# Hedgehog attention and an ELU layer on one core: the first batch written in beats, all five engines in program order

## The chip, the core and the metric

The kernel runs on one core of one Trainium2 chip. The core has five engines with a queue each: TensorE (PE; its weight loads are shown apart as PEld), VectorE (DVE), ScalarE (ACT), GpSimd (POOL) and SyncE (SP), which here only issues transfers. Transfers are carried by DMA engines that all queues share. The metric is the device time of one launch in microseconds; lower is better.

## The reference

For 8 batches and 8 heads, with 576 tokens of 64 features each, q and k are projected with one weight matrix to 128 features. The largest absolute value of each token's projection is subtracted before both exponentials are taken. An output token is a quotient of two sums over the keys. The result goes, as 4608 tokens of 512 features, through a layer of 2048 hidden units with an ELU.

```python
def phi(x):
    proj = np.einsum('bhsd,df->bhsf', x, w_phi)
    proj = proj - np.max(np.abs(proj), axis=-1, keepdims=True)
    return np.concatenate([np.exp(proj), np.exp(-proj)], axis=-1)
q_p, k_p = (phi(q), phi(k))
kv = np.einsum('bhsf,bhsd->bhfd', k_p, v)
z = np.sum(k_p, axis=2)
num = np.einsum('bhsf,bhfd->bhsd', q_p, kv)
den = np.einsum('bhsf,bhf->bhs', q_p, z)[..., None] + 1e-06
...
h = x @ w_in
g = np.where(h > 0.0, h, alpha * (np.exp(np.minimum(h, 0.0)) - 1.0))
return (g @ w_out).astype(np.float32)
```

q, k and v are 8 x 8 x 576 x 64, w_phi 64 x 128, w_in 512 x 2048, w_out 2048 x 512, all float32; the kernel computes its matrix products in bfloat16.

## The kernel before

**Attention in quads.** A quad is four heads of a batch: 512 tokens of each as "main" part, 64 as "tail". There are 16 quads, two per batch, called q0 to q15 here. `attention_steps(i)` returns the steps of quad i: `tr` brings k and q to feature-major order (tiles kT and qT; for i < 3 by TensorE transposes and a copy out of PSUM, for later quads by transposing DMAs on SP's queue); `k` projects the keys of one head at a time (PSUM tile pk), DVE takes the largest absolute value (m_k), ACT the two exponentials (EK); `scale` and `vs` scale the values by exp of m_k (em, vs); `q` does the largest value for the queries (m_q); `qf` their exponentials (Eq); `kv` multiplies EK and vs; `out` multiplies Eq and kv, and DVE combines the two signs (tot); the last out step also divides (den, rec, x); `x` brings x to feature-major order for the layer (xT, and xT_tail for the tails).

**The layer in pieces.** A chunk is the 512 main tokens of a batch; a ninth chunk holds all tails. `mm1(ch, jt)` makes one of 16 column tiles of the hidden layer: four matmuls into PSUM (ph), then ACT's exp (e_sb), POOL's subtraction (u_sb) and DVE's min and max (gT). `mm2(ch, tt, part)` makes a quarter of the product for one of four token tiles tt: four matmuls into PSUM (po); after the fourth quarter ACT copies po to o_sb and SP stores it. The list `pieces` holds them in order, 32 per chunk: 16 mm1 with the last 8 quarters (tt 2 and 3) of the chunk before put in between, then the 8 quarters of tt 0 and 1. A chunk's pieces begin when its number is in `ready`.

**Two regimes.** Quads q0 and q1 and the transposes of q2 are written as one list of steps before manual scheduling starts. There `post` runs its function at once, and the framework's scheduler decides the order on each engine. From q2 on the kernel is in beats: the order on all engines is the program's. Each beat writes one piece of the layer and the steps that `slot_beats` gives it; 16 beats make a slot, a slot holds the k and q half of one quad and the kv and out half of the quad before. `post(lag, fn, rank)` puts work on another engine some beats later, sorted by rank within a beat. Chunk 0 is ready at the first beat, chunk 1 at the 52nd.

**PSUM.** There are eight banks: four for attention (`apsum`, tag ap), three for ph (`mpsum`, tag mp), one for po (`opsum`, tag op). The next po can start only when ACT has copied the last one.

**Loads.** k, q, w_in and w_out are loaded by POOL's queue, which casts to bfloat16; v of batch 0 by POOL too, later v by SP. In the trace an issue on POOL waits for the eighth issue before it to land.

Of the kernel before, what the change touches and what calls it, by code (L numbers as in the profile page):

```python
# [8 lines left out]
FP32 = mybir.dt.float32  # L9
# [13 lines left out]
def kernel(  # L23
# [104 lines left out]

    beat = [0]
    agenda = {}  # L130
    in_beats = [False]
# [15 lines left out]
    def attention_steps(i):  # L147
# [3 lines left out]
        def transposes(n):  # L151
# [4 lines left out]
            if i < 3:  # L156
                tr = apsum.tile([P, 8, P], BF16, name="tr", tag="ap")
# [3 lines left out]
                copy = nc.scalar.copy if n == 1 and b == 0 else nc.vector.tensor_copy  # L161
                copy(dst[:, 0:8, :], tr)
                trt = apsum.tile([P, P], BF16, name="trt", tag="ap")
                nc.tensor.transpose(trt, src[:, t0:t0 + P], ident)
                copy(dst[:, 8, :], trt)
# [14 lines left out]
        def project(xT, hh, m):  # L180
# [4 lines left out]
            for j in range(n):  # L185
# [9 lines left out]
                1,  # L195
# [21 lines left out]
        def k_head(hh):  # L217
            pk = project(st["kT"], hh, st["m_k"])
            if hh < 4:
                exps(pk, lambda sg: st["EK"][:, hh, sg, :], 2)  # L220
            else:
                exps(pk, lambda sg: st["EKt"][:, sg, :], 2)

        def q_head(hh):
            project(st["qT"], hh, st["m_q"])


        eng = nc.vector if i == 1 else nc.gpsimd

        def k_scale():  # L230
# [6 lines left out]
            eng.tensor_copy(vs[:, :, :, D], em)  # L237

        def v_scaled(sg, c):
# [7 lines left out]
            eng.tensor_tensor(  # L247
# [17 lines left out]
        def q_features_tail():  # L265
# [13 lines left out]
            def weights():  # L279
                st["w"] = small.tile([P, 2 * NS], FP32, name="w")  # L280
                nc.scalar.activation(st["w"], st["m_q"], ACT.Exp, scale=2.0)

            post(2, weights, 6)
# [92 lines left out]
        def divide():  # L376
# [5 lines left out]
            for c in range(2):  # L382
                r = slice(c * NS, (c + 1) * NS)
                nc.vector.tensor_tensor(  # L384
                    st["x"][:, :, c, :],
                    st["tot"][:, r, 0:D],
                    rec[:, r, None].to_broadcast((P, NS, D)),
                    op=ALU.mult,
                )

        def x_out():
# [11 lines left out]
            tr = apsum.tile([P, 8, P], BF16, name="tr", tag="ap")  # L403
            for j in range(8):
                nc.tensor.transpose(tr[:, j, :], x[:, j * P:(j + 1) * P], ident)
            nc.vector.tensor_copy(main, tr)
# [267 lines left out]
```

## Time and profile before

| | |
|---|---|
| time, median of 3 runs | 448.89 us (445.23 to 450.13) |
| time of the profiled execution | 446.22 us |
| its span | 444.4 us |
| PE busy | 378.0 us (85%) |
| DVE busy | 284.5 us (64%) |
| ACT busy | 266.7 us (60%) |
| POOL busy | 213.3 us (48%) |
| read from HBM, written to it | 36.77 MB, 9.44 MB |

The profile shows one execution: busy time per engine, the span in 40 slices of 11.1 us with each engine's busy share in tenths, the TensorE clock that was granted, DMA traffic, and groups of instructions with what ended the idle time before them. A row of the timeline begins with start and duration in us. A row of a table by stage has the stage, its length, and for each engine the busy time and the number of instructions, then the granted clock, the DMA engines' busy share and GB/s.

### The profile page before, as it was taken

Reading aid. Unit: us, or ns where it says so; the run is one execution under the profiler, and the core shown is the slowest. Engines: PE = TensorE matmul, PEld = TensorE weight load, DVE = VectorE, ACT = ScalarE, POOL = GpSimd, SP = SyncE. Lnnn points to the kernel's source line nnn. Section 1 sums busy time; section 2 is a strip of 40 time slices with the busy share of each in tenths; the row PEclk is TensorE's granted clock in tenths of the full one; section 3 lists DMA queues with packets and bytes.
Section 4 is the critical chain, followed back from the end, with each engine's and each line's share of the span. In section 5 each row is a group of like instructions: output and inputs, shape, how many; then the busy total and the mean of one; then the engine's idle time right before and its main releaser. Section 6 shows DMA issues by size and latency. Waiting matters only on the chain.

```text
span 444.4 us, 7930 instructions
## 1 busy us (share of the span) xinstructions
PE 378.0 (85%) x2888; PEld 203.7 (46%) x2888; DVE 284.5 (64%) x552; ACT 266.7 (60%) x585; POOL 213.3 (48%) x325
## 2 busy tenths in 40 slices
PE   2575687965989898989898989898999899989985
PEld 2353434543545454535454545454555444434432
DVE  2665676767597768765977687768776763523410
ACT  2953187766668576857685768486848533434511
POOL 9562177544186527742774277436434621423400
PEclk9955699995899999999999999999999999999999
DMA  8899995099309972994199419941521202010023
GB/s 135 158 172 212 226 153 78 23 125 204 70 11 178 159 125 24 108 232 107 21 182 155 112 29 202 139 103 43 63 62 39 50 25 75 27 47 24 25 53 65
DMA packets 93720, 44.89 MB, mean 101 GB/s; under 512 B 62545, under 2 KB 88273, under 8 KB 93681
## 3 DMA queue, kind: packets, MB, share of 16 engines
q1 hardware_dynamic: 65136, 29.57, 33.3%
q0 software_dynamic: 28544, 14.82, 25.2%
q8 instruction: 22, 0.36, 0.3%
q14 instruction: 18, 0.14, 0.1%
HBM read 36.77 MB, written 9.44 MB: 104 GB/s over the span
## 4 chain that ended last, share of the span: by engine, by line
PE 63%; DVE 13%; ACT 11%; DMA 5%; issue 4%; POOL 3%; POOLq 0%; ACTq 0%
PE ph L436 24%; PE po L469 23%; PE pk L186 5%; ACT Eq L212 4%; PE pkv L293 4%; DMA qT<-q_b 4%; DVE x L384 3%; ACT EK L212 3%; DVE gT L455 3%; PE pq L256 2%; ACT o_sb L479 2%; PE pn L326 2%; PE pkv L305 1%; DVE m_q L196 1%; DVE m_k L196 1%
## 5 line engine op out<-in xcount | busy, mean ns | idle before, releaser
L448 POOL TENSOR_SCALAR u_sb<-e_sb 128x512 bf16<-128x512 f32 x144 | 91.4, 636 | 161.9 <-ACT e_sb L445 155.6
L469 PE MATMUL po<-w_out_sb,gT 128*128 128x512 bf16 x576 | 142.4, 379 | 12.2 <-ACT o_sb L479 12.2
L436 PE MATMUL ph<-xT,w_in_sb 128*128 128x512 bf16 x512 | 131.6, 384 | 15.8 <-DVE gT L455 15.4
L445 ACT ACTIVATE e_sb<-ph 128x512 f32<-128x512 f32 x144 | 87.0, 606 | 68.0 <-PE ph L436 65.8
L455 DVE SCALAR_TENSOR_TENSOR gT<-u_sb,ph 128x512 bf16<-128x512 bf16 x144 | 97.4, 682 | 44.0 <-POOL u_sb L448 43.2
L469 PEld LDWEIGHTS <-gT 128*128 128x128 bf16 x576 | 55.4, 98 | 70.2 <-issue 16.1
L436 PEld LDWEIGHTS <-w_in_sb 128*128 128x128 bf16 x576 | 54.3, 98 | 71.1 <-issue 23.5
L212 ACT ACTIVATE Eq<-pq 128x512 bf16<-128x512 f32 x128 | 68.9, 605 | 29.6 <-PE pq L256 29.0
L196 DVE TENSOR_REDUCE m_k<-pk 128x4 f32<-128x512 f32 (+1 forms) x80 | 50.3, 635 | 45.0 <-PE pk L186 44.8
L212 ACT ACTIVATE EK<-pk 128x512 bf16<-128x512 f32 x128 | 69.7, 624 | 11.5 <-DVE m_k L196 11.3
L247 POOL TENSOR_TENSOR vs<-v_b,em 128x512 bf16<-128x512 f32 (+1 forms) x90 | 72.9, 827 | 0.0
L196 DVE TENSOR_REDUCE m_q<-pk 128x4 f32<-128x512 f32 (+1 forms) x80 | 50.6, 635 | 26.4 <-PE pk L186 26.4
L479 ACT COPY o_sb<-po 128x512 f32<-128x512 f32 x36 | 21.3, 591 | 40.0 <-PE po L469 34.3
L186 PE MATMUL pk<-w_phi_both,qT 128*128 128x256 bf16 x144 | 30.8, 290 | 8.2 <-DMA qT<-q_b 4.3
L186 PE MATMUL pk<-w_phi_both,kT 128*128 128x256 bf16 x144 | 30.4, 289 | 5.6 <-DVE m_q L196 2.0
L326 PEld LDWEIGHTS <-Eq 128*128 128x128 bf16 x512 | 25.9, 101 | 16.8 <-issue 4.6
L338 DVE TENSOR_TENSOR tot<-pn,w 128x260 f32<-128x260 f32 x64 | 27.1, 425 | 9.7 <-ACT kv L313 5.1
L326 PE MATMUL pn<-kv,Eq 128*128 128x65 bf16 x512 | 28.6, 199 | 3.1 <-DVE tot L338 1.3
L344 DVE TENSOR_TENSOR tot<-tot,pn 128x260 f32<-128x260 f32 x64 | 27.0, 425 | 1.9
L256 PE MATMUL pq<-qT,w_phi_both 128*128 128x512 bf16 x64 | 25.2, 407 | 0.6 <-ACT Eq L212 0.6
L293 PEld LDWEIGHTS <-EK 128*128 128x128 bf16 x512 | 21.6, 102 | 6.7 <-ACT EK L212 2.3
L186 PEld LDWEIGHTS <-kT 128*128 128x128 bf16 x144 | 14.7, 103 | 20.0 <-issue 6.5
(61 smaller groups left out, 263.2 us busy)
## 6 DMA issues: line engine op xcount, KB each, us to landing
out_dram<-o_sb SPq DMA_DIRECT2D x32, 256.0 KB, 2.4
v_b<-in_v_dram SPq DMA_DIRECT2D x7, 1024.0 KB, 10.6
k_b<-in_k_dram POOLq DMA_DIRECT2D x7, 512.0 KB, 7.9
q_b<-in_q_dram POOLq DMA_DIRECT2D x7, 512.0 KB, 12.0
w_in_sb<-in_moe_w_in_dram POOLq DMA_DIRECT2D x8, 256.0 KB, 7.6
w_out_sb<-in_moe_w_out_dram POOLq DMA_DIRECT2D x8, 256.0 KB, 16.7
v_b<-in_v_dram POOLq DMA_DIRECT2D x2, 512.0 KB, 6.5
out_dram<-o_sb SPq DMA_DIRECT2D x8, 128.0 KB, 2.4
```

The source lines that it names most:

```text
L186: nc.tensor.matmul(pk[:, 2 * j:2 * j + 2, :].rearrange("p a b -> p (a b)"), xT[:, 2 * hh + j, :], w_phi_rhs, start=True, stop=True,)
L196: lambda: nc.vector.tensor_reduce(m[:, o:o + NT] if hh < 4 else m[:, NS - 1::NS], pk[:, 0:2 * n, :], axis=AX.X, op=ALU.max, apply_absolute ...
L212: lambda sg=sg: nc.scalar.activation(dst(sg), psum, ACT.Exp, scale=1.0 - 2.0 * sg),
L247: eng.tensor_tensor(st["vs"][:, sg, r, 0:D], kqv[b][2][:, o:o + n * D].rearrange("p (n d) -> p n d", d=D), st["em"][:, sg, r, None].to_bro ...
L256: nc.tensor.matmul(pq, w_phi_both[:, par, :], st["qT"][:, 4 * c:4 * c + 4, :].rearrange("p a b -> p (a b)"), start=True, stop=True,)
L293: nc.tensor.matmul(pkv[:, c, sg, :], st["EK"][:, 2 * c + s, sg, t * F:(t + 1) * F], st["vs"][:, sg, c * NS + s * NT + t, :], start=first, ...
L326: nc.tensor.matmul(pt[:, t, :], st["Eq"][:, par, c, sg, o:o + P], st["kv"][:, s, c, sg, :], start=True, stop=True,)
L436: nc.tensor.matmul(ph, w_in_sb[:, ct, jt * P:(jt + 1) * P], xTs[ch][:, ct, :] if ch < B else xT_tail[:, ct // 2, :, ct % 2, :], start=(ct ...
L445: post(1, lambda: nc.scalar.activation(e_sb, ph, ACT.Exp), 0)
L448: lambda: nc.gpsimd.tensor_scalar(u_sb, e_sb, -1.0, 1.0, op0=ALU.add, op1=ALU.mult),
L455: lambda: nc.vector.scalar_tensor_tensor(gTs[ch][:, jt, :], u_sb, 0.0, ph, op0=ALU.min, op1=ALU.max),
L469: nc.tensor.matmul(po, gTs[ch][:, jt, tt * P:(tt + 1) * P], w_out_sb[:, jt, :], start=(jt == 0), stop=(jt == N_JT - 1),)
```

## The change

The first three quads are written in beats too, and manual scheduling starts before the first instruction. The hand-written table gives each step of q0 to q2 a beat: the slot of q3 starts at beat 39, chunk 0 is ready at beat 29 and chunk 1 at beat 75, where the beats before q2's slot had no number in the kernel before. From the slot of q4 on the table is the old one.

- Chunk 0 has eight more empty places in the list of pieces, one behind each mm2 quarter.
- w_in is loaded in eight parts as before, but each part is one half of the columns for two row tiles. Batch 0's second k half is loaded ahead of q and v.
- kT and qT of q3 and q4 are made by TensorE and a copy, as those of q0 to q2 are; their PSUM tiles lie in the ph or po banks. The copies of q0's and q1's qT are DVE's and no longer ACT's; q2's kT copy and q0's xT copy are ACT's and no longer DVE's.
- For q0 and q1 the exponentials of a key head stand one beat ahead of its largest value, no longer behind it.
- vs of q1 is POOL's work and no longer DVE's. x of q0 (the two multiplications behind the division) is POOL's, a beat after the division.
- po of tt 1 lies in a ph bank. When attention is over, all po lie in the four attention banks.

```diff
-    def load_w_in(ct, c):
+    def load_w_in(half, g, c):
+        j = slice(half * (DFF // 2), (half + 1) * (DFF // 2))
         nc.gpsimd.dma_start(
-            out=w_in_sb[c * D:(c + 1) * D, ct, :], in_=w_in_r[ct // 2, c, ct % 2]
+            out=w_in_sb[c * D:(c + 1) * D, 2 * g:2 * g + 2, j],
+            in_=w_in_r[g, c, :, :, j].rearrange("s d j -> d s j"),
         )
...
     def post(lag, fn, rank=5):
-        if in_beats[0]:
-            agenda.setdefault(beat[0] + lag, []).append((rank, fn))
-        else:
-            fn()
+        agenda.setdefault(beat[0] + lag, []).append((rank, fn))
...
-            if i < 3:
-                tr = apsum.tile([P, 8, P], BF16, name="tr", tag="ap")
+            if i < 5:
+
+                pool, tag = (opsum, "op") if i in (2, 3) else (mpsum, "mp")
+                tr = pool.tile([P, 8, P], BF16, name="tr", tag=tag)
...
+                copy = nc.scalar.copy if i == 2 and n == 0 else nc.vector.tensor_copy
+                post(1, lambda: copy(dst[:, 0:8, :], tr), 0)
+                post(1, lambda: copy(dst[:, 8, :], trt), 0)
...
         def k_head(hh):
-            pk = project(st["kT"], hh, st["m_k"])
+
+            lag = 2 if i < 2 else 1
+            pk = project(st["kT"], hh, st["m_k"], lag)
             if hh < 4:
-                exps(pk, lambda sg: st["EK"][:, hh, sg, :], 2)
+                exps(pk, lambda sg: st["EK"][:, hh, sg, :], 3 - lag)
...
-        eng = nc.vector if i == 1 else nc.gpsimd
...
-            eng.tensor_tensor(
+            nc.gpsimd.tensor_tensor(
                 st["vs"][:, sg, r, 0:D],
...
-            for c in range(2):
...
+            def x_heads():
+                for c in range(2):
+                    r = slice(c * NS, (c + 1) * NS)
+                    (nc.gpsimd if i == 0 else nc.vector).tensor_tensor(
...
+            if i == 0:
+                post(1, x_heads, 8)
+            else:
+                x_heads()
...
         if part == 0:
-            pos[ch, tt] = opsum.tile([P, DM], FP32, name="po", tag="op")
+
+            pool, tag = opsum, "op"
+            if not attending[0]:
+                pool, tag = apsum, "ap"
+            elif tt == 1:
+                pool, tag = mpsum, "mp"
+            pos[ch, tt] = pool.tile([P, DM], FP32, name="po", tag=tag)
...
-        pieces += [(ch, tt, part) for tt in (0, 1) for part in range(4)]
+        for tt in (0, 1):
+            for part in range(4):
+                pieces.append((ch, tt, part))
+                if ch == 0:
+                    pieces.append(None)
...
+    put(0, (16, 17, 18, 19, 20), q0["out"])
...
+    put_later(0, (29,), [lambda: ready.add(0)], 1)
...
+    put_later(0, (1, 2), load_kq(1, 0), 9)
+    put_later(0, (3, 4, 13, 13), w_in_loads[0], 9)
+    put_later(0, (18,), [hold_v], 9)
+    put_later(0, (19,), [lambda: load_v(1)], 9)
+    put_later(0, (20, 21), load_kq(1, 1), 9)
+    put_later(0, (23, 24, 25, 26), w_in_loads[1], 9)
+    put_later(0, (28, 29, 30, 31), w_out_loads[:4], 9)
+    put_later(0, (38, 40, 42, 44), w_out_loads[4:], 9)
...
+    START = 39
...
```

On POOL's queue before, from the third w_in load to the first work of the layer, vs is that of q0 only, and all loads of batch 1 and of w_out stand in a row:

```order
L81 DMA w_in_sb<-in_moe_w_in_dram 64x2048 x3
L237 CAST vs<-em 128x36
L247 TENSOR_TENSOR vs<-v_b,em 128x8x64 x4
L247 TENSOR_TENSOR vs<-v_b,em 128x2x64
L81 DMA w_in_sb<-in_moe_w_in_dram 64x2048
L247 TENSOR_TENSOR vs<-v_b,em 128x2x64
L81 DMA w_in_sb<-in_moe_w_in_dram 64x2048 x4
L107 DMA k_b<-in_k_dram 128x8x256
L117 DMA k_b<-in_k_dram 64x4x64 x2
L107 DMA q_b<-in_q_dram 128x8x256
L117 DMA q_b<-in_q_dram 64x4x64 x2
L86 DMA w_out_sb<-in_moe_w_out_dram 128x2x512 x8
```

The same place on POOL's queue after the change, from q1's em on:

```order
L236 CAST vs<-em 128x36
L246 TENSOR_TENSOR vs<-v_b,em 128x2x64
L82 DMA w_in_sb<-in_moe_w_in_dram 64x2x1024 x2
L246 TENSOR_TENSOR vs<-v_b,em 128x8x64 x4
L246 TENSOR_TENSOR vs<-v_b,em 128x2x64 x2
L109 DMA q_b<-in_q_dram 128x8x256
L119 DMA q_b<-in_q_dram 64x4x64 x2
L383 TENSOR_TENSOR x<-tot,rec 128x9x64 x2
L82 DMA w_in_sb<-in_moe_w_in_dram 64x2x1024 x4
L88 DMA w_out_sb<-in_moe_w_out_dram 128x2x512 x3
L454 TENSOR_SCALAR u_sb<-e_sb 128x512
L88 DMA w_out_sb<-in_moe_w_out_dram 128x2x512
```

The vs of q1 and the x of q0 have come onto POOL, between loads, and the last loads stand among the layer's u_sb.

On DVE before, from the first m_q of q1 to the middle of q0's out steps, the names with numbers are the PSUM tiles of one out step:

```order
L196 TENSOR_REDUCE m_q<-pk 128x4
L237 CAST vs<-em 128x36
L585 COPY v_b<-em 128x1 x2
L247 TENSOR_TENSOR vs<-v_b,em 128x8x64
L338 TENSOR_TENSOR tot<-pn_384,w 128x260
L196 TENSOR_REDUCE m_q<-pk 128x4
L344 TENSOR_TENSOR tot<-tot,pn_379 128x260
L338 TENSOR_TENSOR tot<-pn_402,w 128x260
L247 TENSOR_TENSOR vs<-v_b,em 128x8x64
L344 TENSOR_TENSOR tot<-tot,pn_397 128x260
```

On DVE after the change, from the end of q0's out steps into those of q1:

```order
L341 TENSOR_TENSOR tot<-tot,pn_438 128x260
L362 TENSOR_TENSOR tot<-pnt,w 128x2x65
L368 TENSOR_TENSOR tot<-tot,pnt 128x2x65
L376 TENSOR_SCALAR den<-tot 128x18
L377 RECIPROCAL rec<-den 128x18
L335 TENSOR_TENSOR tot<-pn_546,w 128x260
L341 TENSOR_TENSOR tot<-tot,pn_541 128x260
```

The vs and the m_q of q1 no longer stand among q0's out steps, and between the division of q0 and the first out step of q1 no x stands on DVE; `tot` has one buffer, so that step waits for POOL's x.

On PE before, in the steady part, where token tile 0 of a chunk ends and token tile 1 begins (with the engines that a row waits for):

```order
L268 LDWEIGHTS w_phi_both
L268 MATMUL pq<-qT,w_phi_both 128x128 [waits Activation_49]
L268 LDWEIGHTS w_phi_both
L268 MATMUL pq<-qT,w_phi_both 128x128
L469 LDWEIGHTS gT
L469 MATMUL po<-w_out_sb,gT 128x512 [waits Activation_49]
```

The same place on PE after the change:

```order
L267 LDWEIGHTS w_phi_both
L267 MATMUL pq<-qT,w_phi_both 128x128 [waits Activation_49]
L267 LDWEIGHTS w_phi_both
L267 MATMUL pq<-qT,w_phi_both 128x128
L482 LDWEIGHTS gT
L482 MATMUL po<-w_out_sb,gT 128x512
```

The order is the same, and the first matmul of tile 1 no longer waits for ACT.

More of the change, by code (lines that the diff above doesn't have):

```diff
@@ L581, in load_v @@
[L581 to L590 removed]
+    w_in_loads = [
+        [
+            lambda half=half, g=g, c=c: load_w_in(half, g, c)
+            for g in range(2)
+            for c in range(2)
+        ]
+        for half in range(2)
@@ L642 @@
+    last = max(at)
+    while beat[0] <= last or pieces or agenda:
+        if beat[0] > last:
+            attending[0] = False
+            if B - 1 in ready:
+                ready.add(B)
+        moe_piece()
+        for f in at.get(beat[0], []):
+            f()
         next_beat()
-        moe_piece()
 _INS = ['q', 'k', 'v', 'w_phi', 'moe_w_in', 'moe_w_out']
```

222 lines of the change are left out of this document (107 added, 115 removed).

## The prediction

> **What bounds the kernel now.** I read the slices of the page first, then the busy time by stage.
>
> ```profile
> span 444.4 us, 7930 instructions
> PE   2575687965989898989898989898999899989985
> PEclk9955699995899999999999999999999999999999
> core 0: us, PE busy (x) PEld busy (x) DVE busy (x) ACT busy (x) POOL busy (x), PEclk, DMA share, GB/s
> 0.00:54.20 54.20, 29.88 (x282) 20.82 (x283) 30.01 (x70) 23.65 (x55) 28.21 (x47) 0.74 1.06 179
> 54.20:91.70 37.50, 31.99 (x222) 16.66 (x220) 25.73 (x48) 27.54 (x62) 25.86 (x39) 0.96 0.64 85
> 91.70:113.80 22.10, 13.84 (x139) 8.61 (x138) 17.22 (x36) 13.12 (x33) 7.18 (x11) 0.72 1.12 177
> 201.20:245.00 43.80, 40.78 (x339) 22.39 (x338) 33.22 (x66) 31.22 (x70) 24.28 (x36) 1.00 0.68 119
> 372.90:444.40 71.50, 62.83 (x286) 27.82 (x285) 22.02 (x32) 25.08 (x43) 19.75 (x32) 0.99 0.15 45
> ```
>
> From the eleventh slice on PE is at 8 or 9 tenths; in the first ten (111 us) it is mostly at 5 to 7. The fourth stage is one steady batch: PE busy 40.78 of 43.80 us (93%). The last stage is the tail, with PE as the bound. The first three stages are the ramp, where no engine is a bound: PE 75.7 of 113.8 us, DVE 73.0, ACT 64.3. The timeline gives its marks:
>
> ```profile
> 6.68 0.69 DVE L162 COPY kT<-tr 128x1024 bf16<-128x1024 bf16 x1 [2.81 <-PE tr L160]
> 54.24 1.06 PE L436 MATMUL ph<-xT,w_in_sb 128*128 128x512 bf16 x2
> 113.75 0.61 PE L436 MATMUL ph<-xT,w_in_sb 128*128 128x512 bf16 x1
> ```
>
> DVE's work starts at 6.7 us, the layer in earnest at 54.2 us (chunk 0, beat 1), and chunk 1 at 113.75 us (beat 52). From chunk 1 on the table of beats is the same in both kernels. The ramp's term is therefore where chunk 1's first ph (now beat 75) falls.
>
> **The ramp.** DVE has most to do once its order is free of waits, so I count DVE's work up to chunk 1: 30.01 + 25.73 + 17.22 = 72.96 us before. Rows of DVE and ACT in the first stage price what moves:
>
> ```profile
> L384 DVE TENSOR_TENSOR x<-tot,rec 128x576 bf16<-128x576 f32 x4 | 2.9, 755 | 0.1
> L247 DVE TENSOR_TENSOR vs<-v_b,em 128x512 bf16<-128x512 f32 x4 | 2.7, 687 | 0.0
> L247 DVE TENSOR_TENSOR vs<-v_b,em 128x128 bf16<-128x128 f32 x2 | 0.6, 297 | 0.0
> L162 DVE COPY kT<-tr 128x1024 bf16<-128x1024 bf16 x3 | 2.1, 688 | 2.9 <-PE tr L160 2.8
> L165 DVE COPY kT<-trt 128x128 bf16<-128x128 bf16 x3 | 0.7, 219 | 0.8 <-PE trt L164 0.8
> L162 ACT COPY qT<-tr 128x1024 bf16<-128x1024 bf16 x2 | 2.0, 1012 | 8.3 <-PE tr L160 8.1
> ```
>
> - q1's vs leaves DVE: 2.7 + 0.6 = -3.3 us. x of q0 leaves it: half of four, -1.5 us.
> - A pair of copies (main and tail) is 0.69 + 0.22 = 0.91 us. q0's and q1's qT come from ACT (+1.8), q3's and q4's kT and qT come from the transposing DMAs (+3.6), q2's kT and q0's xT go to ACT (-1.8).
> - Sum: 72.96 - 3.3 - 1.5 + 1.8 + 3.6 - 1.8 = 71.8 us. ACT exchanges two pairs of copies for two, so its 64.3 us stay.
>
> Now the share of the time in which DVE can work. The ends are a steady batch, where PE sets the pace (33.22 of 43.80: 76%), and the best ramp stretch:
>
> ```profile
> 30.00:40.00 10.00, 4.61 (x43) 3.29 (x43) 8.80 (x23) 0.22 (x1) 3.52 (x5) 0.50 1.32 224
> 60.00:70.00 10.00, 8.23 (x40) 3.77 (x39) 6.79 (x12) 9.47 (x23) 9.46 (x15) 1.00 1.39 171
> 90.00:100.00 10.00, 6.42 (x80) 3.95 (x79) 7.06 (x14) 6.13 (x15) 3.94 (x6) 1.00 1.20 136
> 100.00:110.00 10.00, 5.95 (x49) 3.08 (x46) 8.09 (x18) 6.43 (x17) 4.95 (x7) 0.58 1.08 213
> ```
>
> DVE reached 88% at 30 to 40 us, and 68% at 60 to 70 us, where ACT was full (9.47 of 10). The new order mixes both kinds of work, so I take the steady batch's 76%, the nearest row to mixed work: 6.7 + 71.8 / 0.76 = 101.2 us. That gains 113.75 - 101.2 = 12.6 us. At 88% chunk 1 would start at 88.3 us (gain 25.5). A second way to count comes near it. For chunk 0's start, beat 29:
>
> ```profile
> 0.74 1.28 ACT L162 ACT_TABLE_LOAD   x1 [0.74 <-PEq L658]
> 9.08 1.03 PE L160 MATMUL tr<-ident,q_b 128*128 128x128 bf16 x8 [0.93 <-DMA q_b<-in_q_dram]
> ...
> 11.41 4.03 ACT L212 ACTIVATE EK<-pk 128x512 bf16<-128x512 f32 x8
> 45.33 0.68 PE L326 MATMUL pn<-kv,Eq 128*128 128x65 bf16 x16 [0.62 <-ACT kv L313]
> ```
>
> ACT had 23.65 - 1.28 = 22.4 us of work for the first two quads. Its first exponential at 11.4 us stood behind a qT copy (1.0 us for its main part) and q's transposes (1.0 us); without them it starts at about 9 and ends near 32 us. q1's out steps, division, x and transposes took from 45.3 to 54.2 us, 9 us; with 2 us for POOL's x, below, chunk 0 starts at about 43 us. The 32 beats of the second stage took 37.5 us, 1.17 each, so 46 more give 43 + 53.9 = 97 us.
>
> What the ramp adds in waits:
>
> - `tot` has one buffer, so DVE's first out step of q1 waits for POOL's x of q0, which stands behind three loads of q. DVE's queue holds q1's whole out part behind it, and chunk 0 waits for that. The row for POOL work of this kind is
>
> ```profile
> L247 POOL TENSOR_TENSOR vs<-v_b,em 128x512 bf16<-128x512 f32 x12 | 12.2, 1039 | 0.0
> ```
>
>   Two of 576 elements: 2 x 1.04 x 576/512 = 2.3 us, against 1.5 us on DVE. It lies in the 24% that I leave idle; without that cover it costs 0.8 us.
> - q3's and q4's transposes add four of these pairs to PE, which has 75.7 us of work in 101 us:
>
> ```profile
> 15.67 0.61 PE L160 MATMUL tr<-ident,q_b 128*128 128x128 bf16 x8
> 16.11 0.22 PE L164 MATMUL trt<-ident,q_b 128*128 128x128 bf16 x1
> ```
>
>   4 x (0.61 + 0.22) = 3.3 us, taken at nothing; 3.3 us if PE were full.
> - w_in's loads have the same bytes. The first half's last parts are issued at beat 13 and needed at beat 29, the second half's at beats 23 to 26 and needed at the ninth mm1, beat 41. Taken at nothing, with 15 beats of attention as cover; beyond that cover each us of lateness is one of chunk 0.
> - A key head's exponentials one beat ahead of its largest value, for q0 and q1, changes which of ACT and DVE reads pk first: the same instructions, taken at nothing, and either way within the share.
> - The transposing DMAs that go (q3, q4) free SP; those of q5 stay, and with them this wait:
>
> ```profile
> 101.67 0.53 SPq L107 DMA_DIRECT2D v_b<-in_v_dram  x1
> 110.63 0.61 PE L186 MATMUL pk<-w_phi_both,qT 128*128 128x256 bf16 x2 [3.34 <-DMA qT<-q_b]
> ```
>
>   From the issue of v to the matmul are 9 us. The two are ten beats apart in both kernels, so at 1.17 us a beat most of the 3.3 us goes, and at 0.9 it stays. I leave it inside the share.
>
> **The po banks.** In a steady batch PE waits for ACT's copy of po twice where mm2 quarters follow each other, and six times in the tail:
>
> ```profile
> L479 ACT COPY o_sb<-po 128x512 f32<-128x512 f32 x36 | 21.3, 591 | 40.0 <-PE po L469 34.3
> ...
> 190.74 1.02 PE L469 MATMUL po<-w_out_sb,gT 128*128 128x512 bf16 x4 [0.66 <-ACT o_sb L479]
> 196.18 1.02 PE L469 MATMUL po<-w_out_sb,gT 128*128 128x512 bf16 x4 [0.57 <-ACT o_sb L479]
>   ACT o_sb L479: 4.1, 6
> ```
>
> The first is token tile 3 to tile 0, both still in the po bank: it stays. The second is tile 0 to tile 1: it goes, six times between chunk 1 and chunk 7. PE is busy 93% there, but other waits can take the place, above all this one for gT:
>
> ```profile
> 175.84 1.02 PE L436 MATMUL ph<-xT,w_in_sb 128*128 128x512 bf16 x4 [1.59 <-DVE gT L455]
> ```
>
> So 6 x 0.57 = 3.4 us at most, none at least; I take 2.7. In the tail nothing but PE is late: with four banks the copy of 0.59 us hides behind 16 matmuls, and all 4.1 us go.
>
> **The sum** is made against the profiled execution, 446.22 us: -12.6 - 2.7 - 4.1 = 426.8 us. The three timed runs have a median of 448.89, and all four times average 447.6, 1.4 above the profiled one; so I forecast 428 us.
>
> **The rivals.**
>
> *Dense ramp.* DVE reaches the 88% of its best stretch: 446.2 - 25.5 - 6.8 + 1.4 = 415 us. For it: ACT and PE have 64 and 79 us in 88. Against: that stretch had ACT at 0.22 of 10.
>
> *The ramp at the steady pace.* A steady beat is 43.80 / 32 = 1.37 us, though PE's load makes it so; 75 of them: 6.7 + 102.8 = 109.5 us, a gain of 4.3, and 446.2 - 4.3 - 6.8 + 1.4 = 436.5 us. For it: the order on each engine is fixed, so a beat costs its fullest engine, and POOL has new work. Against: ramp beats hold no or half the layer's pieces.
>
> *The clock stays low.* In the rows by 10 us the granted clock is 1.00 where PE was busy 6.42 or 8.23 of 10, and 0.50 or 0.58 where it was busy 4.61 or 5.95. A ramp cut into short beats with waits in each could keep PE below that. PE's work from beat 29 to 75 is at full clock about 31.99 x 0.96 + 13.84 x 0.72 = 40.7 us, at half clock 81 us: chunk 1 at 43 + 81 = 124 us, and the time 446.2 + 10.3 - 6.8 + 1.4 = 451 us. Against: 40.7 us in the 58 us from 43 to 101 are 7.0 of 10, above both rows with full clock's lower one. The Trainium skill, page "TensorE: Matmul & The Clock Gate", Part 1, says that the clock has two states only, half and full, and falls back after an idle window of about 3.4 us. By that rule intermediate values are mixtures of time, and the waits of a beat, of which the longest steady one shown is 1.59 us, would not trip it; the forecast stands by the rule as by the rows.
>
> *POOL stalls the layer (the slower side).* Each load on POOL waits for the eighth before it to land, and after the change u_sb, without which no gT and no next ph comes, stands behind the last w_out and batch 2's loads on that queue. Before, the loads waited with nothing behind them:
>
> ```profile
> POOL w_out_sb L86 <- DMA q_b<-in_q_dram: 6.8, 3, 5.4
> POOL w_out_sb L86 <- DMA k_b<-in_k_dram: 3.5, 3, 2.7
> ```
>
> If five of the loads behind beat 19 (there are 21) waited like the longest, 5.4 us, on the path, chunk 1 would start 27 us later than forecast, at 128 us: 446.2 + 14.5 - 6.8 + 1.4 = 455 us. It decides from 12.6 + 6.8 + 4.5 = 24 us of such waits on. Against: these waits came where the DMA engines were full (224 GB/s at 30 to 40 us), with all loads issued at once; now they stand over 50 beats.
>
> *The banks do nothing* (PE still waits for ACT in the tail, the copies come late for another reason): 4.1 + 2.7 us less gain, 434 us.
>
> **How the numbers follow.** Forecast, 420 to 433 us: 0.50. Dense ramp: 0.16. Steady pace: 0.18. Low clock: 0.05. POOL's waits: 0.06. Banks alone failing: 0.05. The range holds the forecast, the dense ramp and the steady pace with a margin of some 3 to 4 us for the run-to-run spread: 412 to 440 us. What a measurement of this kernel can tell from no change is about 1%, 4.5 us. Faster by more: 0.50 + 0.16 + 0.18 + 0.05, less 0.03 for a ramp that is slower still than the steady pace: 0.86. The low clock lies within 1%, with that 0.03: 0.08. Slower: 0.06.
>
> **What would show it.** Chunk 1's first ph at 96 to 106 us and chunk 0's at 40 to 46 us; PE's slices 3 to 9 at 7 or more; DVE's busy time up to chunk 1 near 72 us; no wait of po for ACT in the tail and one, not two, per steady batch; the clock at 0.9 or more from 45 us on. Wrong: chunk 1 later than 110 us, POOL loads with waits of over 2 us and u_sb behind them, clock below 0.7 in chunk 0, or ph waits that grow where the po waits went.

## The result and the profile after

The changed kernel takes 426.92 us, median of 4 runs (425.63 to 428.95), against 448.48 us (445.23 to 450.13) of the kernel before on the same chip: a ratio of 0.9532, 95% interval 0.9466 to 0.9598. The forecast was 428 us. One execution of run 2 below took 498.44 us at a mean granted clock of 0.75, and that run's time and ratio are those of its other five. The changed kernel's profiled execution took 426.87 us. Its page, with PE and the granted clock in 40 slices of 10.6 us:

```profile
span 425.1 us, 7945 instructions
PE   3685878767989998999899989998999898999995
PEclk9887899996999999999999999999999899999999
```

PE's slices 3 to 9 read 8, 5, 8, 7, 8, 7, 6 (7, 5, 6, 8, 7, 9, 6 before). Two of them are below the 7 that was forecast: the ramp is shorter, not dense. The stages of the ramp, cut at the new marks (columns as in the prediction's table):

```profile
0.00:43.10 43.10, 27.50 (x280) 18.48 (x281) 27.60 (x63) 26.09 (x59) 32.55 (x51) 0.86 0.98 174
43.10:82.10 39.00, 31.72 (x267) 18.51 (x271) 30.12 (x60) 27.02 (x63) 31.65 (x47) 0.97 0.79 109
82.10:101.90 19.80, 12.48 (x124) 7.92 (x126) 14.04 (x29) 11.87 (x30) 4.95 (x7) 0.86 1.19 194
```

The marks in PE's timeline are the first ph of chunk 0 and, for chunk 1, the first ph that has a record:

```profile
43.08 0.63 PE L442 MATMUL ph<-xT,w_in_sb 128*128 128x512 bf16 x1
...
101.87 1.41 PE L442 MATMUL ph<-xT,w_in_sb 128*128 128x512 bf16 x3 [0.34 <-issue]
```

The second row has three matmuls where a ph has four, and 0.34 us of idle time that nothing explains: the first matmul's record is missing. Its weight load is recorded at 101.46 us. In the traces where the record is there, chunk 1's first weight load and first matmul start together (113.75 us before), so 101.46 us is the mark of chunk 1; runs 5, 6, 8 and 9 lack the same record and are read in the same way.

In the kernel before, the layer's first two matmuls ran at 41.74 us, and the next ones at 54.24 us. As in the prediction, the second of these is chunk 0's start there, and runs 9 and 11 are read in the same way.

The span is 444.4 - 425.1 = 19.3 us shorter. Three parts make it up. They are read off the first ph matmul of chunks 1 and 7 (chunk 7's is at 372.19 us before and at 357.09 us after; the stages of the prediction and the expectations below put that cut 0.7 us later for before and 1.5 us later for after):

| | before | after | gain | forecast |
|---|---|---|---|---|
| start to chunk 1 | 113.75 us | 101.46 us | 12.3 us | 12.6 us |
| chunk 1 to chunk 7 | 258.4 us | 255.6 us | 2.8 us | 2.7 us |
| chunk 7 to the end | 72.2 us | 68.0 us | 4.2 us | 4.1 us |

Chunk 0 starts 11.2 us earlier (54.24 to 43.08), and from there to chunk 1 it takes 58.4 us instead of 59.5. So nearly the whole gain of the ramp lies ahead of chunk 0. ACT's timeline shows where it was. Before:

```profile
11.41 4.03 ACT L212 ACTIVATE EK<-pk 128x512 bf16<-128x512 f32 x8
...
26.91 0.87 ACT L313 CAST kv<-pkv 128x260 bf16<-128x260 f32 x2
36.16 0.22 ACT L281 ACTIVATE w<-m_q 128x18 f32<-128x18 f32 x1 [8.38 <-DVE m_q L196]
40.44 4.03 ACT L212 ACTIVATE Eq<-pq 128x512 bf16<-128x512 f32 x8 [4.06 <-PE pq L256]
44.27 0.75 ACT L212 ACTIVATE Eqt<-pq 128x256 bf16<-128x256 f32 x2
```

and after:

```profile
8.15 4.03 ACT L212 ACTIVATE EK<-pk 128x512 bf16<-128x512 f32 x8 [6.13 <-PE pk L186]
...
33.98 0.69 ACT L212 ACTIVATE Eqt<-pq 128x256 bf16<-128x256 f32 x2
```

Before, ACT stood from 27.8 to 40.4 us with 0.2 us of work in between, since q1's query exponentials (Eq) were written behind q0's x. After, there is no such hole, the first exponential comes 3.3 us earlier, and the last one of q1 at 34.0 us in place of 44.3.

On the other end, PE's waits from chunk 1 to chunk 7, before (us in total, times, longest):

```profile
PE ph L436 <- DVE gT L455: 10.8, 11, 2.0
PE po L469 <- ACT o_sb L479: 7.5, 12, 0.7
PE pk L186 <- DMA qT<-q_b: 1.0, 1, 1.0
```

and after:

```profile
PE ph L442 <- DVE gT L461: 10.8, 11, 2.0
PE po L482 <- ACT o_sb L492: 4.0, 6, 0.7
PE pk L186 <- DMA qT<-q_b: 0.7, 2, 0.4
```

Six of the twelve waits for po went, as the bank of tt 1 says, and the waits for gT did not grow. In the tail no wait for po is left, and one for xT is new:

```profile
PE ph L442 <- DMA xT<-x: 1.2, 1, 1.2
```

### The profile page after: what moved, and what is told of

Read it like the earlier page. It is cut to its first block, busy times and chain, and to the rows that moved or that the text cites. A ratio compares the mean times of both kernels' runs of the same rounds, so it can differ in the third digit from the quotient of the medians.

```text
span 425.1 us, 7945 instructions
## 1 busy us (share of the span) xinstructions
PE 370.8 (87%) x2877; PEld 202.6 (48%) x2924; DVE 283.2 (67%) x551; ACT 267.0 (63%) x585; POOL 221.1 (52%) x334
## 4 chain that ended last, share of the span: by engine, by line
PE 65%; DVE 14%; DMA 9%; ACT 5%; POOL 3%; issue 3%; ACTq 0%; POOLq 0%; DVEq 0%
PE ph L442 24%; PE po L482 23%; DMA qT<-q_b 7%; PE pk L186 6%; PE pkv L290 3%; DVE gT L461 3%; DVE x L383 3%; PE pq L255 2%; PE pn L323 2%; DVE m_k L196 2%; PE pkv L302 1%; ACT EK L212 1%; DVE m_q L196 1%; ACT Eq L212 1%; POOL vs L246 1%
## 5 line engine op out<-in xcount | busy, mean ns | idle before, releaser
L482 PE MATMUL po<-w_out_sb,gT 128*128 128x512 bf16 x561 | 139.7, 381 | 4.8 <-ACT o_sb L492 4.0
L442 PE MATMUL ph<-xT,w_in_sb 128*128 128x512 bf16 x480 | 127.1, 384 | 18.3 <-DVE gT L461 14.6
L246 POOL TENSOR_TENSOR vs<-v_b,em 128x512 bf16<-128x512 f32 (+1 forms) x96 | 77.8, 829 | 0.0
L323 PEld LDWEIGHTS <-Eq 128*128 128x128 bf16 x512 | 25.0, 99 | 17.5 <-issue 5.6
L290 PE MATMUL pkv<-vs,EK 128*128 128x65 bf16 x512 | 22.4, 198 | 0.7 <-ACT EK L212 0.6
## 6 DMA issues: line engine op xcount, KB each, us to landing
out_dram<-o_sb SPq DMA_DIRECT2D x32, 256.0 KB, 2.5
w_in_sb<-in_moe_w_in_dram POOLq DMA_DIRECT2D x8, 256.0 KB, 7.5
w_out_sb<-in_moe_w_out_dram POOLq DMA_DIRECT2D x8, 256.0 KB, 6.2
```

The source lines that it names most:

```text
L246: nc.gpsimd.tensor_tensor(st["vs"][:, sg, r, 0:D], kqv[b][2][:, o:o + n * D].rearrange("p (n d) -> p n d", d=D), st["em"][:, sg, r, None]. ...
L290: nc.tensor.matmul(pkv[:, c, sg, :], st["EK"][:, 2 * c + s, sg, t * F:(t + 1) * F], st["vs"][:, sg, c * NS + s * NT + t, :], start=first, ...
L323: nc.tensor.matmul(pt[:, t, :], st["Eq"][:, par, c, sg, o:o + P], st["kv"][:, s, c, sg, :], start=True, stop=True,)
L442: nc.tensor.matmul(ph, w_in_sb[:, ct, jt * P:(jt + 1) * P], xTs[ch][:, ct, :] if ch < B else xT_tail[:, ct // 2, :, ct % 2, :], start=(ct ...
L482: nc.tensor.matmul(po, gTs[ch][:, jt, tt * P:(tt + 1) * P], w_out_sb[:, jt, :], start=(jt == 0), stop=(jt == N_JT - 1),)
```

## The experiments

The theory under test is the prediction's: the ramp goes by DVE's work over a share of 76%, and the banks take away one po wait per batch and six in the tail. Where not told otherwise, edits are made to the changed kernel. The marks are the first ph of chunk 0, 1 and 7 in each profiled execution. The runs were made on several chips; the ratio is to the kernel before on the same chip:

| run | time, us | ratio to before, 95% | chunk 0 | chunk 1 | chunk 1 to 7 |
|---|---|---|---|---|---|
| changed kernel | 426.92 | 0.953 [0.947, 0.960] | 43.08 | 101.46 | 255.6 |
| all po in one bank | 434.58 | 0.971 [0.968, 0.975] | 42.52 | 100.97 | 259.1 |
| q1's vs on DVE | 428.02 | 0.959 [0.956, 0.962] | 44.87 | 104.12 | 256.1 |
| qT copies on ACT | 427.44 | 0.955 [0.952, 0.958] | 44.30 | 102.64 | 255.3 |
| q3, q4 by DMA | 433.86 | 0.971 [0.968, 0.974] | 42.40 | 106.26 | 256.3 |
| scheduler's order to chunk 0 | 426.53 | 0.953 [0.949, 0.958] | 43.83 | 101.80 | 255.2 |
| x of q0 on DVE | 425.07 | 0.952 [0.947, 0.957] | 42.08 | 100.39 | 257.6 |
| v behind qT | 426.43 | 0.954 [0.949, 0.958] | 42.55 | 99.41 | 258.7 |
| tt 0 in the ph bank | 427.39 | 0.956 [0.951, 0.960] | 44.49 | 104.71 | 254.9 |
| v late, tt 0, x on DVE | 419.56 | 0.939 [0.936, 0.942] | 42.11 | 99.56 | 251.5 |
| w_in by rows | 430.02 | 0.963 [0.960, 0.966] | 44.26 | 104.49 | 255.3 |
| before, q1's qf early | 445.62 | 0.996 [0.993, 0.999] | 51.71 | 110.62 | 260.9 |
| before, that and vs on POOL | 454.37 | 1.018 [1.014, 1.021] | 62.97 | 122.79 | 256.9 |

Up to chunk 0 the kernels "all po in one bank", "v behind qT" and "tt 0 in the ph bank" are the changed kernel, and yet their chunk 0 lies between 42.5 and 44.5 us. At chunk 1 "tt 0 in the ph bank", which differs up to there only in the banks of po, is 3.3 us later than the changed kernel. So a single profile's mark is good to some 1 to 1.5 us at chunk 0 and perhaps 3 us at chunk 1 (the last section shows why).

**1. All po in one bank.**

```diff
-            if not attending[0]:
-                pool, tag = apsum, "ap"
-            elif tt == 1:
-                pool, tag = mpsum, "mp"
```

> The change with all po in the one po bank, as before. Theory (the waits for ACT's copy are on PE's path): the steady part from chunk 1 to chunk 7 goes from 256.7 to 260.2 us (six waits of 0.57 us more), the tail from 66.5 to 70.6 (4.1 more), chunk 1's first ph stays at 102 us; 7.6 us in all, 434.5 us. Rival (in the steady part waits for gT take over what the banks give): only the tail moves, about 431 us.

PE's waits from chunk 1 to chunk 7, and for po in the tail:

```profile
PE ph L442 <- DVE gT L461: 10.9, 11, 2.0
PE po L478 <- ACT o_sb L488: 7.5, 12, 0.7
...
PE po L478 <- ACT o_sb L488: 4.1, 6, 0.7
```

The waits are back as before. The stretch takes 259.1 us (+3.5) and the tail 72.2 us (+4.2), while the ramp stays; the banks do what was forecast. What a wait costs is more than its idle time. The six of the tail show 4.1 / 6 = 0.68 us each; without them the tail is 4.2 us shorter although the wait for xT has come, so by this estimate they were worth (4.2 + 1.2) / 6 = 0.90 each. Part of the difference is in the rows themselves: four 128x512 matmuls show 1.02 us, and where nothing waits the next row starts 0.86 us after them (171.31 and 172.17 us in the changed kernel). The last 0.16 us counts as busy ahead of a wait, and is overlapped without one.

**2. q1's vs on DVE again.**

```diff
-            nc.gpsimd.tensor_tensor(
+            (nc.vector if i == 1 else nc.gpsimd).tensor_tensor(
```

> The change with the vs of q1 on DVE again, as before the change: 3.3 us more of DVE work in the first 30 us, and POOL that much less. Theory of the prediction (the ramp's length is DVE's work over a share of 0.76): chunk 1 starts 4.3 us later, at 106 us, time about 431 us. Rival (the ramp is set by a chain of single waits, and DVE's work as such is not on it): chunk 1 stays within 1.5 us of 102 us.

The small cast of em into vs went to DVE too. Chunk 1 came 2.7 us later, between the two, and the time is 1.1 us longer with intervals that overlap. A mark can't tell 2.7 us from 4.3 or from nothing for certain, so this run does not decide.

**3. qT copies of q0 and q1 on ACT.**

```diff
-                copy = nc.scalar.copy if i == 2 and n == 0 else nc.vector.tensor_copy
+                copy = nc.scalar.copy if (i == 2 and n == 0) or (i < 2 and n == 1) else nc.vector.tensor_copy
```

> The change with the copies of q0's and q1's qT on ACT again: DVE 1.8 us less, ACT 2.6 us more. DVE's share as the measure: chunk 1 2.4 us earlier, about 99.5 us, time 424.5. Rival, ACT paces the first 43 us: chunk 0 and with it chunk 1 up to 2.6 us later, 429.5 us. Rival, single waits: no more than 1 us either way.

Less work for DVE, and chunk 1 was 1.2 us later, not 2.4 earlier. Run 1 is the nearer comparison: it has the changed kernel's code up to chunk 0, and its granted clock went through the same states as here (half for 10.2 us, full for 17.1, half for 3.4, then full for 51.2; from 13.7 us on there and from 15.6 us on here). Chunk 0 and 1 stood at 42.52 and 100.97 us there, and are 1.8 and 1.7 us later here. Of the 2.6 us more of ACT's work most shows up, as the rival *ACT paces the first 43 us* has it.

**4. q3 and q4 by transposing DMAs.**

```diff
-            if i < 5:
+            if i < 3:
```

> The change with kT and qT of q3 and q4 by transposing DMAs again: DVE 3.6 us less, PE 3.3 us less, SP 8 transfers more. DVE's share: chunk 1 4.8 us earlier, 97 us, time 422. Rival (transposing DMAs bring waits of 3 to 7 us each, as q5's does now with 4.1 us): chunk 1 at 105 to 109 us, time 430 to 434 us.

PE's wait for qT up to chunk 1:

```profile
PE pk L186 <- DMA qT<-q_b: 5.9, 1, 5.9
```

DVE has 3.6 us less to do, and chunk 1 is 4.8 us later, the time 6.9: the sign is against the theory of DVE's share, and the rival's numbers hold. The four pairs of transposes that the prediction put on PE at nothing are what keeps the stretch from chunk 0 to chunk 1 at 58.4 us; by DMA it is 63.9.

**5. The scheduler's order up to chunk 0.** The table of beats stays, manual scheduling begins only at beat 29.

```diff
-    ctx.enter_context(
-        tc.manual_schedule(engines={E.PE, E.DVE, E.Activation, E.Pool, E.SP})
-    )
...
+        if beat[0] == 29:
+            ctx.enter_context(
+                tc.manual_schedule(
...
```

> The change with manual scheduling starting at beat 29 and no longer at the first instruction: the same steps, written in the same beats, but up to chunk 0 the framework's scheduler decides the order on the engines, as in the kernel before. Theory (the program's order is what brings chunk 0 forward): chunk 0 starts at 50 to 55 us, and chunk 1 at 108 to 113, time about 434 to 438. Rival (the table of beats is enough, the scheduler makes about the same of it): chunk 0 at 43 to 45 us, time within 2 us of 427.

No mark differs by more than the spread, although the scheduler's order is not the table's (on DVE, for one, the first largest value of the keys stands behind the second kT copy and no longer ahead of it). What brings chunk 0 forward lies in the steps as the table writes them; that the engines are held to this order is worth nothing here.

**6. x of q0 on DVE.**

```diff
-                    (nc.gpsimd if i == 0 else nc.vector).tensor_tensor(
+                    nc.vector.tensor_tensor(
...
-            if i == 0:
-                post(1, x_heads, 8)
-            else:
-                x_heads()
+            x_heads()
```

> The change with x of q0 on DVE again, right behind the division. Theory of single waits (DVE's 2.4 us wait for POOL's x is on the path): it goes, 1.4 us of DVE work comes: chunk 0 and chunk 1 about 1 us earlier, time 426. DVE's share as the measure: 1.5 us more DVE work, chunk 1 2 us later, 429.

DVE has 1.5 us more work, and the layer starts 1.0 us earlier. The wait that this takes away, in DVE's and POOL's timeline of the changed kernel:

```profile
34.42 0.43 DVE L335 TENSOR_TENSOR tot<-pn,w 128x260 f32<-128x260 f32 x1 [2.37 <-POOL x L383]
...
32.13 2.25 POOL L383 TENSOR_TENSOR x<-tot,rec 128x576 bf16<-128x576 f32 x2 [2.88 <-DVE rec L377]
```

POOL's x took 2.25 us as forecast, and DVE stood for all of it. Both the mark and the time (425.07 with an interval that holds the changed kernel's) move by about what the mark's spread is, so the size is open; the runs show no gain from this part of the change.

**7. v behind qT on SP's queue.**

```diff
-            put(s0, (6,), [lambda nb=nb: load_v(nb)])
+            put(s0, (10,), [lambda nb=nb: load_v(nb)])
```

> The change with the load of v, from q4's slot on, four beats later, so that it stands behind the transposing DMAs of qT on SP's queue and no longer ahead of them. Theory (v's megabyte ahead of them is what makes PE wait 4.1 us for q5's qT): the wait goes, chunk 1 starts at 97.5 to 98.5 us, the steady part is 0 to 0.7 us shorter, time 422.5 to 424. Rival (the k and q loads of POOL's queue fill the DMA engines just the same): at least half of the wait stays, time 425 or more. Other rival: v then delays the next slot's kT, and a wait of 1 us or more for kT or xT appears in each batch.

What stood there, in SP's and PE's timeline of the changed kernel:

```profile
89.63 0.38 SPq L109 DMA_DIRECT2D v_b<-in_v_dram  x1
...
92.68 2.81 SPq L167 DMA_TRANSPOSE qT<-q_b  x1
...
98.35 0.61 PE L186 MATMUL pk<-w_phi_both,qT 128*128 128x256 bf16 x2 [4.12 <-DMA qT<-q_b]
```

and in this run:

```profile
99.41 0.61 PE L442 MATMUL ph<-xT,w_in_sb 128*128 128x512 bf16 x1
101.85 1.01 PE L442 MATMUL ph<-xT,w_in_sb 128*128 128x512 bf16 x2 [1.83 <-DMA xT<-x]
```

The first ph came 2.1 us earlier and the second stood for xT, which now lay behind the same megabyte of v. The stretch from chunk 1 to 7 grew by 3.1 us, 1.8 of it this wait; the granted clock was half until 107.9 us, in the changed kernel until 103.1. The wait had moved, and nothing was gained.

**8. tt 0 in the ph bank in place of tt 1.**

```diff
-            elif tt == 1:
+            elif tt == 0:
```

> The change with po of token tile 0, and no longer tile 1, in a ph bank. Tiles 1, 2 and 3 share the po bank, with two mm1 between them or a whole tile 0. Theory: PE's remaining six waits of 0.66 us, tile 3 to tile 0, go too and no new one comes: the steady part 256.7 to about 252.5 us, time 423. Rival (ph waits longer for its bank because a po holds one while the next chunk begins, or the waits for gT take it over): steady part 255 us or more.

PE's waits from chunk 1 to chunk 7:

```profile
PE ph L442 <- DVE gT L461: 10.9, 11, 2.0
PE pk L186 <- DMA qT<-q_b: 4.2, 4, 2.0
```

No wait for po is left, but those for qT went from 0.7 to 4.2 us, and the stretch is 254.9 us: 4.0 us of waits taken away, 0.7 gained. By the cut that the expectation used, 1.5 us later, it went from 256.7 to 256.0 us: the number of the rival, but for another reason than the two that it gave. The suspect is v ahead of the transposes on SP's queue; run 10 tries it.

**9. The kernel before, with q1's qf steps early.**

```diff
-    steps += b["vs"][5:] + a["x"] + b["qf"]
+        steps += b["qf"][j:j + 1]
+    steps += b["vs"][5:] + a["x"]
```

> The kernel before with one edit in its list of steps: q1's query features stand one by one among q0's out steps, and no longer behind q0's x, behind which PE waited 3.8 us while ACT had nothing to do. It asks what in the table of beats brought chunk 0 forward. Theory (it is that q1's exponentials no longer wait for q0's end): chunk 0's start in earnest goes from 54.2 to about 51 us, chunk 1's from 113.8 to about 111, time 3 us less than before. Rival (the loads or DVE's work of that stretch set the pace): chunk 0 within 1 us of 54.2.

Chunk 0 came 2.5 us earlier, chunk 1 3.1, and the time is 1.3 us less. One later batch took 47.5 us in place of 44.7 and gave as much back: PE waited 2.1 us for a qT there where it was 1.0 before, and the clock was half for 3.4 us from 196.4 us on. ACT's hole is filled (its last Eqt of q1 starts at 36.21 us), which is 8 us earlier for ACT but not for the layer. DVE's timeline shows the next link:

```profile
27.36 0.69 DVE L196 TENSOR_REDUCE m_q<-pk 128x4 f32<-128x512 f32 x1 [3.45 <-PE pk L186]
...
28.31 0.68 DVE L247 TENSOR_TENSOR vs<-v_b,em 128x512 bf16<-128x512 f32 x1
28.91 0.42 DVE L338 TENSOR_TENSOR tot<-pn,w 128x260 f32<-128x260 f32 x1
...
37.16 1.43 DVE L384 TENSOR_TENSOR x<-tot,rec 128x576 bf16<-128x576 f32 x2
```

From 27.4 to 38.6 us DVE has no idle time shown: q1's m_q and vs stand between q0's tot.

**10. v late, tt 0 in the ph bank, x of q0 on DVE.** The three edits of 6, 8 and (at beat 18) 7 together.

```diff
-            put(s0, (6,), [lambda nb=nb: load_v(nb)])
+            put(s0, (18,), [lambda nb=nb: load_v(nb)])
```

> The change with three edits together: v's load 12 beats later, behind the next xT transposes and the qT ones; po of token tile 0 in a ph bank in place of tile 1's; x of q0 on DVE. Theory (each batch loses 0.73 us per po wait, and the waits for qT and xT that showed up in its place come from v's load ahead of them): chunk 1 at 98 to 100 us, batches of 42.1 us each, time about 417 to 419 us. Rival (the DMA engines, and not the place in SP's queue, set the steady pace once the po waits are gone): waits for qT, kT or v move but stay, batches of 42.8 us or more, time 423 or more.

419.56 us, 0.939 of the kernel before and some 7 us less than the changed kernel. Chunk 1 started at 99.56 us, and three of the batches took 42.0 us. PE's waits from chunk 1 to chunk 7:

```profile
PE ph L439 <- DVE gT L458: 10.9, 11, 2.0
PE ph L439 <- DMA xT<-x: 1.3, 1, 1.3
```

The waits for po and for qT are both gone. This settles run 8: the gain had been there, and v's place on SP's queue had taken it. The DMA engines, the rival, had the same bytes to move. What v's place at beat 18 is worth without the bank was not tried.

**11. The kernel before, with qf early and q1's vs on POOL.**

```diff
-        eng = nc.vector if i == 1 else nc.gpsimd
+        eng = nc.gpsimd
```

> The kernel before with the two ramp edits that the earlier runs priced: q1's qf steps among q1's q, out and vs steps (as in the run that had that alone: chunk 0's first ph at 51.71 us, chunk 1's at 111.03, 445.6 us), and now q1's vs on POOL as well. Theory: the ramp's gain is the sum of a few single links of a chain that goes from engine to engine; q1's vs stand on DVE in that chain (rows of q0's out steps and q1's vs alternate there at 28 to 37 us), six multiplications of 0.69 and 0.30 us, 3.3 us in all; so chunk 0 starts at 48 to 49.5 us and chunk 1 at 108 to 109.5. Rival 1: POOL's vs take 1.04 us each, 7 us for q1, behind those of q0, and the kv sums of q1 wait for them: chunk 0 at 51 us or later, no gain. Rival 2: the gain comes at chunk 0 but is lost again before chunk 1, as part of it was in the earlier run's second batch: chunk 1 at 111.

Against run 9 chunk 0 was neither 3 us earlier nor the same, but 11.3 us later, and the kernel 1.8% slower than the one before. POOL's and PE's timeline:

```profile
35.89 0.35 POOL L237 CAST vs<-em 128x36 bf16<-128x36 f32 x1
...
44.34 0.71 POOL L86 DMA_DIRECT2D w_out_sb<-in_moe_w_out_dram  x1 [6.21 <-DMA q_b<-in_q_dram]
...
48.05 4.76 POOL L247 TENSOR_TENSOR vs<-v_b,em 128x512 bf16<-128x512 f32 x6
...
49.16 0.60 PE L293 MATMUL pkv<-vs,EK 128*128 128x65 bf16 x8 [7.47 <-POOL vs L247]
```

The scheduler put the cast among the issues of w_out and q1's multiplications behind the last of them, and those issues wait for loads to land. From the cast at 35.89 to the first product at 48.05 are 12 us. That is the mechanism of the rival *POOL stalls the layer*, in the kernel before. What the table of beats gains here it gains on POOL's queue: it says which loads stand ahead of vs.

**12. w_in by rows in the changed kernel.**

```diff
-        j = slice(half * (DFF // 2), (half + 1) * (DFF // 2))
+        ct = 2 * half + g
...
-            out=w_in_sb[c * D:(c + 1) * D, 2 * g:2 * g + 2, j],
-            in_=w_in_r[g, c, :, :, j].rearrange("s d j -> d s j"),
+            out=w_in_sb[c * D:(c + 1) * D, ct, :], in_=w_in_r[ct // 2, c, ct % 2]
```

> The changed kernel with w_in loaded in whole rows of one column tile, as before, in the same eight places of the table of beats (the first ph then needs the first column tile's loads whole, and the last of its four column tiles lands only with the loads of beats 23 to 26, issued at 34 to 37 us). Theory (w_in's halves are worth nothing, as the prediction took them): chunk 0 at 42 to 45 us, chunk 1 at 101 to 104, time 425 to 429. Rival: the halves are what lets chunk 0 start: the load issued at about 36.5 us takes 7.5 us to land (the median of w_in's loads), so the first ph, which sums over all column tiles, cannot end before 44 us and chunk 0 starts at 45 to 47, with chunk 1 2 to 4 us later than 101.9, 429 to 431 us.

```profile
44.26 1.49 PE L441 MATMUL ph<-xT,w_in_sb 128*128 128x512 bf16 x3
46.47 0.58 PE L441 MATMUL ph<-xT,w_in_sb 128*128 128x512 bf16 x1 [0.72 <-DMA w_in_sb<-in_moe_w_in_dram]
```

The fourth matmul of the first ph waits 0.72 us for its rows, which the halves avoid, and the time is 3 us longer than the changed kernel's, with ratios whose intervals just meet. But the marks are those of run 8, which loads w_in in halves, and the profiled executions of both, at the same mean clock of 0.952, took 429.6 us here and 429.34 there. What the halves are worth stays open between next to nothing and 3 us.

## Why the prediction was right, and where it was not

**The time.** 428 us forecast, 426.92 measured; the three terms came out at 12.3, 2.8 and 4.2 us for 12.6, 2.7 and 4.1, 19.3 for 19.4 in all. That all three are so near is in part luck, as the next paragraphs show.

**The ramp's term: right number, wrong step.** "DVE's work over a share of 76%" gave 101.2 us, and measured were 101.46 us, 27.60 + 30.12 + 14.04 = 71.76 us of DVE's work (71.8 forecast) and a share of 71.76 / (101.46 - 6.7) = 76%. That looks like a proof and is none: runs 2, 3, 4 and 6 changed DVE's work by +3.3, -1.8, -3.6 and +1.5 us, for which the step says +4.3, -2.4, -4.8 and +2.0 us; chunk 1 moved by +2.7, +1.2, +4.8 and -1.1. Three of the four have the other sign. Runs 2 and 6 alone would be inside the spread; run 4 is far outside it, and run 3 has run 1 as a neighbour with the same clock. So DVE's amount of work does not set the ramp. What fits the runs is a chain that goes from engine to engine, in which each edit counts by the link it makes or breaks: in the profile's chain up to 102 us the largest part of any line is 9.6% (PE's pk), followed by the layer's ph with 7.7%, ACT's EK with 5.8% and DVE's m_k with 5.6%.

**The second count was nearer the mechanism.** It followed ACT's exponentials and q1's out part to chunk 0 at 43 us; measured 43.08. The path bears out: ACT was busy 21.73 of the 26.52 us from its first exponential to the last one of q1, and run 3 shows that more work for ACT there costs most of its length. The exact hit is luck: q1's exponentials ended at 34.7 us in place of 32, and from there to chunk 0 it took 8.4 us in place of 11. Its second half, 46 beats of 1.17 us, was short: 58.4 us were taken, 1.27 each. Of the 12.3 us the runs give single parts: q1's vs on POOL up to 2.7 (run 2), q3's and q4's transposes on TensorE 4.8 (run 4), x of q0 on POOL about -1 (run 6); in the kernel before, qf early 3.1 (run 9) and qf early with vs on POOL -9 (run 11). Such parts don't add up, since each only shows the next late link. What each of the rest (k's second half ahead of q and v, EK ahead of m_k, the xT copy on ACT) is worth was not tried alone and stays open, and with it what most of the 11.2 us ahead of chunk 0 is made of.

**q5's qT** was put "inside the share", with most of 3.3 us expected to go. It stayed, with 4.12 us: v was issued 8.7 us ahead of the matmul, about as before (9.0), so the ten beats took 0.87 us each and not 1.17.

**The edits taken at nothing.** The transposes on PE are worth 4.8 us against DMAs; w_in's halves between next to nothing and 3; the program order alone, nothing (run 5).

**The banks.** 2.7 us forecast for the steady part, 2.8 measured, and 3.5 by run 1. In a batch without other waits the distance between the first weight loads of two chunks went from 43.52 to 42.80 us, 0.72 for the one wait that shows 0.57; six of them make 4.3 us, more than the 3.4 that the prediction held for the most. Two things lowered it. Two waits for qT, 0.7 us in all, stand in the changed kernel and not in run 1. And in the last batch the clock was half for 3.4 us:

```profile
331.76:335.18 3.42, 1.40 (x9) 0.63 (x8) 3.28 (x8) 2.17 (x7) 2.52 (x4) 1.00 0.00 0
335.18:338.59 3.41, 3.41 (x9) 1.21 (x9) 1.26 (x3) 0.60 (x1) 0.62 (x1) 0.50 0.58 128
```

PE waits 2.02 us for gT in the first of these rows. The kernel before has the same wait at 349 us, but no half clock behind it; its last batch took 38.7 us, and run 1's, with the same waits as before and a half clock at 338 us, 40.4. So this cost some 1.7 us, which no term of the prediction had.

In the tail "nothing but PE is late" failed: the waits were worth some 5.4 us, not 4.1, and the wait for xT took 1.2 of it, so that the sum came out right by two misses.

**The rivals.** *Dense ramp* and *ramp at the steady pace* needed chunk 1 at 88 and 109.5 us. *The clock stays low*: it was 0.97 in the second stage; in the third it was 0.86, below the 0.9 that was given as a sign. That the waits of a beat would not bring the clock down, as the prediction argued from the rule that it cites, did not hold: with a wait of 2.02 us in the row from 331.76 us above it fell. *The banks do nothing* falls with run 1. *POOL stalls the layer*: in the changed kernel POOL's loads stood for no longer than this:

```profile
POOL w_out_sb L88 <- DMA q_b<-in_q_dram: 0.7, 1, 0.7
POOL k_b L109 <- DMA q_b<-in_q_dram: 0.6, 1, 0.6
```

The reason given against it, loads spread over 50 beats, holds; run 11 shows that the danger was real.

## What to carry to other kernels

In a stage where no engine is full, follow the chain (which instruction waits for which, and what comes next when that wait goes) and price edits by their links; a total of busy time over a plausible share can hit the number and still give the wrong sign for three edits of four. When a wait is taken away, look at once for the transfer that is issued just in time behind a large one on the same queue: here it took the whole gain until it was moved too (runs 7, 8 and 10). Work on a queue that also issues loads is only as early as the loads ahead of it. And before two profiles are compared to a microsecond, lay their granted clock side by side.

## What was unexpected of the hardware

**Equal ramps differ by the clock's phase.** The changed kernel and run 8 have the same instructions up to chunk 0. The granted clock is full or half, and in these traces it changes only at steps of 3.41 us. Cut at the steps, stretches of the changed kernel (columns as above: PE's busy time comes behind the length, the granted clock stands third from the end):

```profile
28.01:31.42 3.41, 3.36 (x47) 2.52 (x47) 1.73 (x5) 2.03 (x6) 1.24 (x2) 0.50 0.84 113
31.42:34.84 3.42, 1.93 (x37) 1.54 (x35) 0.98 (x4) 2.50 (x6) 2.71 (x3) 1.00 1.20 250
34.84:38.25 3.41, 3.20 (x39) 2.64 (x39) 2.82 (x8) 0.72 (x1) 3.35 (x6) 0.50 1.29 276
```

and of run 8:

```profile
28.31:31.73 3.42, 3.34 (x43) 2.27 (x42) 1.70 (x5) 1.95 (x6) 1.52 (x3) 0.50 0.62 141
31.73:35.14 3.41, 2.56 (x34) 2.28 (x33) 0.82 (x4) 1.90 (x5) 2.40 (x3) 0.50 1.23 256
35.14:38.55 3.41, 2.83 (x36) 2.49 (x36) 2.69 (x7) 0.89 (x4) 3.41 (x6) 0.50 1.37 230
38.55:41.97 3.42, 2.15 (x18) 1.16 (x16) 2.50 (x8) 2.27 (x4) 0.96 (x2) 0.50 1.12 289
41.97:45.38 3.41, 2.03 (x13) 1.57 (x15) 3.41 (x7) 1.67 (x4) 0.00 (x0) 0.50 1.13 214
45.38:48.79 3.41, 3.41 (x14) 1.69 (x14) 0.67 (x2) 2.40 (x5) 1.29 (x2) 0.50 1.20 198
```

In the changed kernel the clock changes at every step here; in run 8 it stays at half for six, and chunk 0 starts 1.4 us later, chunk 1 3.3 us. The rows show what brings the full clock back: it follows a step at half clock in which PE was busy nearly throughout (3.36 and 3.20 us; in run 8 only the last, 3.41 us), and not one with PE busy 2.03 to 2.83 us. Over the fourteen traces of this case, of 60 steps at half clock with PE busy 90% or more 58 were followed by full clock, and of 70 with less 67 by half; the first row of run 8 (3.34 us) is one of the two that differ. The way down is less sharp: the full clock was lost only behind steps with PE busy 72% or less, and kept behind some with as little as 43%. So the same wait can cost clock or not, by where the steps cut it: the wait of 2.02 us for gT did in the changed kernel and did not in the kernel before.

Over runs of one kernel the mean clock and the time go together: of run 8's executions the one at 0.983 took 425.18 us, the one at 0.952 429.34. The Trainium skill, page "TensorE: Matmul & The Clock Gate", Part 1, names a window of about 3.4 us that runs free of the kernel, and two states; the steps agree. It also has the full clock come back after one busy window of that length. The 58 of 60 agree with that; PE busy 80% in the mean, 16.32 of 20.49 us in run 8's six rows, was not enough, as all but the first and the last of them held too much idle time.

**A wait on PE costs more than its idle time**: by estimate 0.90 us for 0.68 shown in the tail, and 0.7 for 0.57 in a steady batch.
